# Last unit's stores moved into the else branch of the flag test, and its first copy from ScalarE to VectorE

## The chip, the cores and the metric

The kernel runs on 1 core of one Trainium2 chip. The metric is device time in microseconds (us) of one launch. The kernel before was run four times: 572.84, 571.76, 571.29 and 570.13 us, median 571.53 us.

## The reference

A gated linear recurrence over 768 tokens (4 batches, 8 heads, 48 values a head) feeds a two-layer network with an ELU between the layers. Cut to what is computed:

```python
f = 1.0 / (1.0 + np.exp(-f_logit))
state = np.zeros((B, H, D, D))
for t in range(S):
    state = f[:, :, t, :, None] * state + einsum('bhd,bhe->bhde', k[:, :, t], v[:, :, t])
    y[:, :, t] = einsum('bhd,bhde->bhe', q[:, :, t], state)
x = y.transpose(0, 2, 1, 3).reshape(B * S, H * D)     # 3072 x 384
h = x @ w_in                                          # 384 x 2048
g = np.where(h > 0, h, np.exp(np.minimum(h, 0)) - 1)
out = g @ w_out                                       # 2048 x 384
```

## The kernel before

The 3072 rows of the output are cut into 12 units of 256 tokens (`NU` = 12). `fast` does the whole computation: for each unit the recurrence as chunked matrix products, and then the network in 8 pairs of column blocks (`NP` = 8): `up` makes a pair's hidden values, `elu` the activation, `down` adds the pair's part of the second product into PSUM. The loop at L1134 runs over the steps of all units in an order written out by hand; `down` trails `up` by two pairs (`LAG`). This order stands in a manual schedule that ends with `start.close()` at L1153, behind the last `down`.

From the third unit on both products are done with seven half-size products in the place of eight. For the second product this leaves four PSUM banks (`pm[0]` to `pm[3]`, each 128 x 384, used as two halves of 192), and at a unit's last pair (`j == NP - 1`, L979 to L998) they are put together: ScalarE copies a half of bank 0 into SBUF tile `u2` (L986), and five VectorE additions (the helper at L985, called at L987 to L991) make from it, from the tile `u43` and from the banks the 256 x 384 result `o`. Each addition but the last two uses what the one before wrote. The result goes to DRAM in four stores of 96 KB (L992 to L997), one for each half of the columns of each 128 rows. SyncE's queue issues them; for the last unit the two stores of the second 128 rows go through ScalarE's queue. `o` is a tile of pool `sb` with two buffers, used by the units in turn.

`fast` also checks that its inputs allow its shortcuts. Late in the last unit the check ends in one number, `flag` (L1017 and L1018), 128 when all is well. At L1162 each engine loads it from SBUF into a register, and at L1163 each engine tests it on its own: below 128 the slower kernel `general` runs and writes everything once more; otherwise every engine jumps over `general`'s instructions. L1163 is also the line of the semaphore instructions that follow the jump and bring the engine's semaphores to the values that `general` would have left. L1193 is the end of the program: SyncE waits for every semaphore, all engines meet, and the semaphores are cleared.

What sets the order around the change is each engine's own program order: on an engine, the load of `flag` and the jump stand behind all that `fast` issues on it. For SyncE and ScalarE that includes the last unit's stores.

Of the kernel before, what the change touches and what calls it, by code (L numbers as in the profile page):

```python
# [8 lines left out]
FP32 = mybir.dt.float32  # L9
# [344 lines left out]


@with_exitstack
def fast(ctx: ExitStack, tc: tile.TileContext, q, k, v, f_logit, w_in, w_out, out, flag):

# [15 lines left out]
    nc = tc.nc  # L376
    B, H, D, S = q.shape
    DM = H * D
# [3 lines left out]
    U = 256  # L382
# [3 lines left out]
    NU = B * UPB  # L386
# [5 lines left out]
    DH = DM // 2  # L392
# [22 lines left out]
    sb = ctx.enter_context(tc.tile_pool(name="sb", bufs=2))  # L415
# [54 lines left out]
    for y in first_y:  # L470
# [7 lines left out]
        out=causal[:], in_=causal[:], compare_op=ALU.is_ge, fill=0.0, base=0,  # L478
# [450 lines left out]
    def elu(P):  # L929
# [5 lines left out]
        if m >= DIRECT:  # L935
            s = ss[P] = sb.tile([128, 4, 128], FP32, tag="sums", name=f"sums{m}_{j}", bufs=3)
            a = [[g[:, i, t * 128 : (t + 1) * 128] for i in range(2)] for t in range(2)]
            for i, x, y, op in (
# [2 lines left out]
            ):  # L941
                nc.gpsimd.tensor_tensor(out=s[:, i], in0=x, in1=y, op=op)  # L942

    def down(P):
        m, j = order[P]
        if j == 0:
            pms[m] = [ps.tile([128, DM], FP32, tag=f"m{i + 2 * (m == 1)}", name=f"psM{m}_{i}") for i in range(NW if m < DIRECT else 4)]
        pm, g = pms[m], gs.pop(P)
        ends = dict(start=(j == 0), stop=(j == NP - 1))
        if m < DIRECT:  # L950
            for i in range(2):
                for t in range(NW):
                    nc.tensor.matmul(  # L953
                        pm[t][:], lhsT=g[:, i, t * 128 : (t + 1) * 128], rhs=wo[:, 2 * j + i, :],
                        start=(j == 0 and i == 0), stop=(j == NP - 1 and i == 1),
                    )
            if j == NP - 1:
                o = sb.tile([128, 2, DM], FP32, tag="o", name=f"o{m}")
                for t in range(NW):
                    nc.scalar.copy(o[:, t], pm[t][:])  # L960
                    t0 = m * U + t * 128
                    nc.sync.dma_start(out=out[t0 : t0 + 128, :], in_=o[:, t])
                del pms[m]
            return
        s = ss.pop(P)
        a = [[g[:, i, t * 128 : (t + 1) * 128] for i in range(2)] for t in range(2)]
        b = [[wo[:, 2 * j + i, h * DH : (h + 1) * DH] for h in range(2)] for i in range(2)]
        c = [combos[:, i, j] for i in range(4)]

        for bank, half, x, y in (  # L970
            (0, 0, a[0][0], b[0][0]), (3, 0, a[0][1], b[1][0]), (0, 1, s[:, 1], c[1]),
            (1, 0, s[:, 0], c[0]), (1, 1, s[:, 2], c[2]), (2, 1, a[1][1], c[3]), (2, 0, s[:, 3], b[1][1]),
        ):
            first = j == 0 and (bank, half) in ((0, 0), (3, 0), (1, 0), (2, 1))
            nc.tensor.matmul(  # L975
                pm[bank][:, half * DH : (half + 1) * DH], lhsT=x, rhs=y,
                start=first, stop=(j == NP - 1), skip_group_check=True,
            )
        if j == NP - 1:  # L979
            p = [[pm[i][:, h * DH : (h + 1) * DH] for h in range(2)] for i in range(4)]  # L980
            o = sb.tile([128, 2, DM], FP32, tag="o", name=f"o{m}")
            u2 = sb.tile([128, DH], FP32, tag="u2", name=f"u2_{m}", bufs=1)
            u43 = sb.tile([128, 2, DH], FP32, tag="u43", name=f"u43_{m}", bufs=1)
            flat = o[:].rearrange("p t f -> p (t f)")
            add = lambda to, x, y: nc.vector.tensor_tensor(out=to, in0=x, in1=y, op=ALU.add)  # L985
            nc.scalar.copy(u2[:], p[0][0])  # L986
            add(flat[:, 0:DH], p[3][0], u2[:])  # L987
            add(u2[:], p[0][1], u2[:])
            add(u43[:], pm[1][:].rearrange("p (h f) -> p h f", h=2), u2[:].unsqueeze(1).broadcast_to([128, 2, DH]))
            add(flat[:, 3 * DH :], p[1][0], u43[:, 1])  # L990
            add(flat[:, DH : 3 * DH], pm[2][:], u43[:].rearrange("p h f -> p (h f)"))  # L991
            for t in range(2):  # L992
                for h in ((1, 0) if t else (0, 1)):
                    (nc.scalar if t and m == NU - 1 else nc.sync).dma_start(
                        out=out[m * U + t * 128 : m * U + (t + 1) * 128, h * DH : (h + 1) * DH],
                        in_=o[:, t, h * DH : (h + 1) * DH],
                    )  # L997
            del pms[m]  # L998

    low = cst.tile([128, 1], FP32, name="low")  # L1000
# [107 lines left out]
    for n in range(1, NFT):  # L1108
        t = max(needs[n][0] - 2, 0)
# [12 lines left out]
    for u in range(3, NU):  # L1122
        t = (u - 1) * NFT
# [4 lines left out]
    for n in range(NR):  # L1128
        t = 3 * NFT + (NU - 4) * NFT * n // NR + RR
# [4 lines left out]
    for T in range(NU * NFT):  # L1134
        P = T // 2
        sevens = order[P][0] >= DIRECT
        if T % 2 and sevens:
            joined(P)
        if T % 2 == 0 and P and order[P - 1][0] < DIRECT:
            elu(P - 1)  # L1140
        for f in plan.pop(T, ()):
            f()
        if T % 2 == 0:
            up(P)
        elif P >= LAG:
            down(P - LAG)
        for n in later.pop(T, ()):
            split(n)
            lower(n)
    elu(NU * NP - 1)  # L1150
    for P in range(NU * NP - LAG, NU * NP):
        down(P)
    start.close()  # L1153


def kernel(tc, q, k, v, f_logit, w_in, w_out, out):

    nc = tc.nc
    with tc.tile_pool(name="flags", bufs=1) as pool:
        flag = pool.tile([1, 1], I32, name="flag")  # L1160
        fast(tc, q, k, v, f_logit, w_in, w_out, out, flag)
        seen = nc.values_load(flag[0:1, 0:1])  # L1162
        with tc.If(seen < 128):  # L1163
            general(tc, q, k, v, f_logit, w_in, w_out, out)


# [30 lines left out]
```

## Time and profile before

| what | value |
|---|---|
| median of four runs | 571.53 us (570.13 to 572.84) |
| the profiled execution's own time | 571.99 us |
| its span, first to last instruction | 570.2 us |
| outside the span | 1.8 us |
| granted TensorE clock, mean | 0.979 |
| TensorE busy | 547.7 us (96%) |
| VectorE / ScalarE / GpSimd busy | 394.6 / 229.6 / 265.6 us |
| last matmul ends | about 563.25 us |
| last VectorE addition ends | 564.68 us |
| from there to the end of the span | 5.5 us |

Busy times are sums over the instructions of an engine; the span runs from the first to the last instruction of any engine, and the time of a run is some 1.8 us more. TensorE is busy nearly throughout. Behind its last matmul stand 6.9 us in which it does nothing, and that is where this change is made. The profile does not count branches, semaphore instructions or DMA issues as busy, so these 6.9 us look nearly empty in the busy figures; they are read from the rows of the lines L1162, L1163 and L1193.

### The profile page before, as it was taken

What the parts mean: (1) busy time and instruction counts of PE and PEld (TensorE: products, weight loads), DVE (VectorE), ACT (ScalarE), POOL (GpSimd) and SP (SyncE); (2) the same over time, 40 slices, a digit from 0 to 9 for tenths busy, and PEclk for the clock granted to TensorE, in tenths of its full rate; (3) what the DMA queues carried; (4) which work ended last, traced back from release to release, by engine and by line L of the source; (5) the groups of instructions that cost most, each with busy time, mean ns of one, the idle gap of its engine ahead of it and who ended that gap; (6) DMA issues with size and microseconds to landing.
All of it is one profiled execution on the core that took longest, in us unless ns stands there. A gap on an engine that the chain in (4) does not pass through costs nothing.

```text
span 570.2 us, 15171 instructions
## 1 busy us (share of the span) xinstructions
PE 547.7 (96%) x6210; PEld 503.6 (88%) x6210; DVE 394.6 (69%) x764; ACT 229.6 (40%) x418; POOL 265.6 (47%) x530
## 2 busy tenths in 40 slices
PE   5688999999999999999999999999999999999995
PEld 2566777778999999999999999999999999999994
DVE  8689476745885785885785885885786786745542
ACT  3287736333443443434333343343333433333331
POOL 6510027642374465465366357257257347325332
PEclk9598999999999999999999999999999999999998
DMA  8989770060025224215216216216216202201001
GB/s 204 250 216 307 183 209 14 2 160 29 2 45 137 65 55 142 78 43 152 79 36 155 85 37 152 85 37 153 84 37 154 84 15 65 86 7 30 29 1 35
DMA packets 37902, 53.27 MB, mean 93 GB/s; under 512 B 3680, under 2 KB 27648, under 8 KB 37824
## 3 DMA queue, kind: packets, MB, share of 16 engines
q1 hardware_dynamic: 37024, 51.62, 34.4%
q8 instruction: 51, 0.84, 0.6%
q10 hardware_dynamic: 800, 0.59, 0.4%
q14 instruction: 27, 0.22, 0.1%
HBM read 44.04 MB, written 4.72 MB: 86 GB/s over the span
## 4 chain that ended last, share of the span: by engine, by line
PE 91%; DMA 4%; DVE 2%; POOL 1%; ACT 1%; issue 1%; ACTq 0%; SPq 0%; DVEq 0%; POOLq 0%
PE psH L878 35%; PE psM L975 33%; PE psM L953 8%; PE psH L923 6%; PE psS L701 2%; PE psY L739 2%; PE psY L759 2%; PE psU_a L724 2%; PE psT L665 2%; DMA area<-in_moe_w_in_dram 1%; DMA f<-f 1%; DMA area<-in_moe_w_out_dram 1%; DMA k<-in_k_dram 1%; ACT area L569 1%; DVE bits L559 0%
## 5 line engine op out<-in xcount | busy, mean ns | idle before, releaser
L878 PE MATMUL psH<-xt,wi 128*128 128x128 f32 (+1 forms) x960 | 177.1, 293 | 0.0
L942 POOL TENSOR_TENSOR sums<-gg 128x128 f32<-128x128 f32 x160 | 69.6, 456 | 210.8 <-DVE gg L932 202.5
L878 PEld LDWEIGHTS psH<-xt,wi 128*128 128x128 f32 x960 | 135.9, 192 | 0.8
L910 ACT ACTIVATE gg<-hh 128x512 f32<-128x512 f32 x80 | 50.4, 631 | 205.9 <-DVE hh L900 138.0
L878 PE MATMUL psH<-xt,area 128*128 128x128 f32 x640 | 110.5, 275 | 0.0
L878 PEld LDWEIGHTS psH<-xt,area 128*128 128x128 f32 x640 | 96.9, 192 | 4.1
L887 DVE TENSOR_TENSOR hh<-psH,u 128x256 f32<-128x256 f32 x80 | 33.8, 423 | 88.6 <-ACT u L885 88.6
L975 PE MATMUL psM<-area,sums 128*128 128x192 f32 x480 | 91.2, 326 | 0.0
L975 PEld LDWEIGHTS psM<-area,sums 128*128 128x128 f32 x480 | 80.1, 190 | 0.2 <-POOL sums L942 0.2
L975 PE MATMUL psM<-wo,gg 128*128 128x192 f32 x320 | 68.1, 335 | 0.0
L617 POOL TENSOR_TENSOR k<-k,f 128x256 f32<-128x256 f32 x48 | 39.1, 817 | 60.0 <-DVE f L622 47.2
L627 DVE RECIPROCAL f<-f 128x256 f32<-128x256 f32 x36 | 62.7, 1747 | 1.3
L911 ACT ACTIVATE gg<-gg 128x512 f32<-128x512 f32 x96 | 60.6, 631 | 3.0
L932 DVE SCALAR_TENSOR_TENSOR gg<-gg,hh 128x512 f32<-128x512 f32 x80 | 55.8, 697 | 1.8 <-ACT gg L911 1.8
L975 PEld LDWEIGHTS psM<-wo,gg 128*128 128x128 f32 x320 | 50.2, 190 | 1.9
L900 DVE TENSOR_TENSOR hh<-psH,u43h 128x256 f32<-128x256 f32 (+1 forms) x160 | 49.8, 352 | 2.7
L923 PE MATMUL psH<-xt,wi 128*128 128x256 f32 x192 | 44.5, 382 | 1.3 <-DVE wi L577 1.1
L942 POOL TENSOR_TENSOR sums<-gg,sums 128x128 f32<-128x128 f32 x80 | 42.7, 534 | 6.3
L953 PE MATMUL psM<-wo,gg 128*128 128x384 f32 x128 | 45.2, 497 | 0.0
L885 ACT COPY u<-psH 128x128 f32<-128x128 f32 x80 | 21.1, 263 | 59.3 <-PE psH L878 59.3
L923 PEld LDWEIGHTS psH<-xt,wi 128*128 128x128 f32 x192 | 36.0, 190 | 8.5 <-issue 1.5
L900 DVE TENSOR_TENSOR u43h<-psH,hh 128x256 f32<-128x256 f32 x80 | 33.9, 423 | 13.3 <-PE psH L878 13.0
(96 smaller groups left out, 721.7 us busy)
## 6 DMA issues: line engine op xcount, KB each, us to landing
area<-in_moe_w_out_dram SPq DMA_DIRECT2D x8, 768.0 KB, 8.4
again<-in_moe_w_in_dram SPq DMA_DIRECT2D x16, 384.0 KB, 4.0
again<-in_moe_w_out_dram SPq DMA_DIRECT2D x16, 384.0 KB, 3.4
k<-in_k_dram SPq DMA_DIRECT2D x12, 384.0 KB, 5.0
q<-in_q_dram SPq DMA_DIRECT2D x12, 384.0 KB, 5.6
v<-in_v_dram SPq DMA_DIRECT2D x12, 384.0 KB, 6.0
area<-in_moe_w_in_dram SPq DMA_DIRECT2D x8, 576.0 KB, 7.8
out_dram<-o SPq DMA_DIRECT2D x38, 96.0 KB, 1.7
```

What stands on the lines that cost most here:

```text
L617: e.tensor_tensor(out=t[n][:, p], in0=t[n][:, p], in1=t["f"][:, p, "kq".index(n)], op=ALU.mult)
L627: nc.vector.reciprocal(f[:, p, 1], f[:, p, 0])
L878: nc.tensor.matmul(to, lhsT=lhs, rhs=rhs, start=(n == 0), stop=True, skip_group_check=True)
L887: add = lambda to, x, y: nc.vector.tensor_tensor(out=to, in0=x, in1=y, op=ALU.add)
L900: add = lambda to, x, y: nc.vector.tensor_tensor(out=to, in0=x, in1=y, op=ALU.add)
L910: nc.scalar.activation(g[:], h, AF.Relu, scale=-1.0)
L911: nc.scalar.activation(g[:], g[:], AF.Exp, scale=-1.0)
L923: nc.tensor.matmul(ph[:, i], lhsT=wi[j][:, kt, i * 128 : (i + 1) * 128], rhs=xts[m][:, kt, :], start=(kt == 0), stop=(kt == NKT - 1),)
L932: nc.vector.scalar_tensor_tensor(out=g[:], in0=g[:], scalar=-1.0, in1=phs.pop(P), op0=ALU.add, op1=ALU.max)
L942: nc.gpsimd.tensor_tensor(out=s[:, i], in0=x, in1=y, op=op)
L953: nc.tensor.matmul(pm[t][:], lhsT=g[:, i, t * 128 : (t + 1) * 128], rhs=wo[:, 2 * j + i, :], start=(j == 0 and i == 0), stop=(j == NP - 1 ...
L975: nc.tensor.matmul(pm[bank][:, half * DH : (half + 1) * DH], lhsT=x, rhs=y, start=first, stop=(j == NP - 1), skip_group_check=True,)
```

## The change

Three things are changed.

The four stores of the last unit are no longer issued in `fast`. `down` puts the function that issues them into the list `left`, `fast` returns it, and the program calls it in an else branch of the flag test. The queues are the same: SyncE for the first 128 rows, ScalarE for the second.

The tile `o` comes from two pools of one buffer each, in turn: from `sb` for units with an even number and from the pool that also holds `flag` for odd ones. That pool lives beyond `fast`, and the last unit, number 11, takes its tile from it.

The copy into `u2` goes to VectorE in the last unit; in the others it stays on ScalarE.

```diff
-def fast(ctx: ExitStack, tc: tile.TileContext, q, k, v, f_logit, w_in, w_out, out, flag):
+def fast(ctx: ExitStack, tc: tile.TileContext, q, k, v, f_logit, w_in, w_out, out, flag, outer):
...
+    left = []
...
-            o = sb.tile([128, 2, DM], FP32, tag="o", name=f"o{m}")
+            o = (outer if (NU - m) % 2 else sb).tile([128, 2, DM], FP32, tag="o", name=f"o{m}", bufs=1)
...
-            nc.scalar.copy(u2[:], p[0][0])
+            (nc.vector.tensor_copy if m == NU - 1 else nc.scalar.copy)(u2[:], p[0][0])
...
-            for t in range(2):
-                for h in ((1, 0) if t else (0, 1)):
-                    (nc.scalar if t and m == NU - 1 else nc.sync).dma_start(
-                        out=out[m * U + t * 128 : m * U + (t + 1) * 128, h * DH : (h + 1) * DH],
-                        in_=o[:, t, h * DH : (h + 1) * DH],
-                    )
+            def store(*queues):
+                for t in range(2):
+                    for h in ((1, 0) if t else (0, 1)):
+                        queues[t].dma_start(
+                            out=out[m * U + t * 128 : m * U + (t + 1) * 128, h * DH : (h + 1) * DH],
+                            in_=o[:, t, h * DH : (h + 1) * DH],
+                        )
+
+            if m == NU - 1:
+                left.append(store)
+            else:
+                store(nc.sync, nc.sync)
...
     start.close()
+    return left[0]
...
-        fast(tc, q, k, v, f_logit, w_in, w_out, out, flag)
+        store = fast(tc, q, k, v, f_logit, w_in, w_out, out, flag, pool)
         seen = nc.values_load(flag[0:1, 0:1])
-        with tc.If(seen < 128):
+        with tc.If(seen < 128) as branch:
             general(tc, q, k, v, f_logit, w_in, w_out, out)
+        with branch.Else():
+            store(nc.sync, nc.scalar)
```

More of the change, by code (lines that the diff above doesn't have):

```diff
@@ L980, in down @@
             p = [[pm[i][:, h * DH : (h + 1) * DH] for h in range(2)] for i in range(4)]
-            o = sb.tile([128, 2, DM], FP32, tag="o", name=f"o{m}")
+            o = (outer if (NU - m) % 2 else sb).tile([128, 2, DM], FP32, tag="o", name=f"o{m}", bufs=1)
             u2 = sb.tile([128, DH], FP32, tag="u2", name=f"u2_{m}", bufs=1)
```

## The prediction

> **What bounds the kernel now.** I read the page first, for what fills the span, then the chain of waits of the last 15 us, then single lines and queues there.
>
> ```profile
> span 570.2 us, 15171 instructions
> PE 547.7 (96%) x6210; PEld 503.6 (88%) x6210; DVE 394.6 (69%) x764; ACT 229.6 (40%) x418; POOL 265.6 (47%) x530
> ```
>
> PE is the bound of the kernel up to its last matmul, and nothing in the change touches a matmul. The chain of waits shows where PE's part ends:
>
> ```profile
> 556.22 7.04 PE psM L975 x42
> 563.26 0.57 DVE u L985
> 563.83 0.02 issue
> 563.86 0.37 DVE o L985
> 564.22 0.19 DVEq L1162
> 564.42 0.26 DVE o L985
> ```
>
> Columns are start, length and what ran. The last matmul ends at 563.26 and the last addition at 564.68; the span ends at 570.2. The chain stops 5.5 us early because what follows is not counted as busy. It is the rows of L1162 (load of the flag), L1163 (jump and semaphores behind it) and L1193 (end of the program) that fill this gap:
>
> ```profile
> L1162 SPq TENSOR_LOAD <-flag x1: 491/491/491, 565.1 to 565.1; - x1
> L1162 ACTq TENSOR_LOAD <-flag x1: 577/577/577, 565.3 to 565.3; - x1
> ...
> L1163 SPq EVENT_SEMAPHORE  x8: 17/17/17, 568.2 to 568.8; - x8
> L1163 POOLq COMPARE_BRANCH  x1: 45/45/45, 561.9 to 561.9; - x1
> L1163 PEldq COMPARE_BRANCH  x1: 3962/3962/3962, 562.5 to 562.5; - x1
> L1163 DVEq COMPARE_BRANCH  x1: 72/72/72, 564.5 to 564.5; - x1
> L1163 POOLq EVENT_SEMAPHORE  x1: 17/17/17, 564.5 to 564.5; - x1
> L1163 SPq COMPARE_BRANCH  x1: 50/50/50, 565.7 to 565.7; - x1
> L1163 ACTq COMPARE_BRANCH  x1: 58/58/58, 565.9 to 565.9; - x1
> L1163 PEldq EVENT_SEMAPHORE  x1: 51/51/51, 566.6 to 566.6; - x1
> L1163 DVEq EVENT_SEMAPHORE  x1: 21/21/21, 567.4 to 567.4; - x1
> L1163 ACTq EVENT_SEMAPHORE  x1: 17/17/17, 568.8 to 568.8; - x1
> ...
> L1193 SPq EVENT_SEMAPHORE  x10: 17/28/28, 568.9 to 570.1; - x10
> ```
>
> The figures are durations in ns (lowest, median, highest) and the first and last start. On every engine 2.6 to 4.1 us lie between the start of the jump and the instruction behind it: POOL 561.9 to 564.5, PE 562.5 to 566.6, DVE 564.5 to 567.4, SP 565.7 to 568.2, ACT 565.9 to 568.8. SP is last where it matters: its jump stands behind its last store (issued at 564.71, 0.33 long) and the flag's load (565.09 to 565.58). Behind the gap SP runs 8 semaphore instructions in 0.60, then 8 more (L1193) in 0.57 to 569.42; from there the meeting of the engines and the clearing take 0.75 to 570.17. ACT is through at 568.85, before SP needs it.
>
> What the stores themselves need is in the DMA view of 561 to 571:
>
> ```profile
> out_dram<-o SPq DMA_DIRECT2D x2, 96.0 KB, 2.8
> out_dram<-o ACTq DMA_DIRECT2D x2, 96.0 KB, 2.5
> ```
>
> The last number is us from issue to landing. By their semaphores the two stores of SP are complete at 566.10 and 567.01, those of ACT at 566.62 and 567.27. All have landed 1 us before SP is back from its jump at 568.25: now **the jump hides the landing**, not the reverse.
>
> **The change, part by part.**
>
> *Stores into the else branch.* The issues are the same four, on the same queues, so no instruction is added for them; they move behind the flag's load and the jump. On SP nothing else is queued between the last store of unit 10 (issued at 533.59) and those of unit 11, and the flag is written at 552.2 (its cast is a 136 ns DVE instruction there). So SP loads the flag at about 552.4, jumps at 553.0 and is in the else branch at 553.0 + 2.6 = 555.6, while the first store is due at 562.7. SP's jump (0.55 from the end of its issue to the jump's start, plus 2.6) leaves the end, covered by 7 us of PE work. If that cover were gone it would cost 3.1 us again. Nothing is queued behind the waiting stores on SP but the end of the program.
>
> On ACT the last activation of the last unit starts at 558.10; the load of the flag (0.58) and the jump can follow, and ACT would be back at about 558.1 + 0.6 + 2.8 = 561.5 to 562.1, whether the load goes beside the activation or behind it. Its first store is due at 564.24. This works only because of the copy's move: with the copy still on ACT (561.99 to 562.31) ACT would be back at 562.0 + 0.6 + 2.8 = 565.4 or later, 1.2 us too late.
>
> PE, POOL and DVE issue no stores; their jumps stay where they are. DVE's is now next in line: it starts at 564.49, DVE is back at 567.40 and ready for the meeting at 567.51.
>
> *The tile in an outer pool.* Two pools of one buffer, used in turn, are the same rotation as one pool of two. No instruction, no wait: 0.
>
> *The copy on VectorE.* Before, ACT's copy starts at 561.99 and the addition waiting for it at 562.34: 0.35. The trace has no DVE copy of 128x192 from PSUM. From below, DVE's cast of one element took 0.136; from above, its addition of 128x192 took 0.358. Between dependent DVE instructions there are 0.105 (562.695 to 562.800). So 0.24 to 0.46 in the place of 0.35. A copy moves as many elements as the addition, so I take 0.45, near the upper row: the whole chain of additions shifts by **+0.10** (bounds -0.11 and +0.11), and the last addition ends at 564.78. DVE was idle for 2.46 us before, so the copy delays no other work.
>
> The row for ACT's copy is 0.300 (median of ten). [...]
>
> *The end.* The last stores are issued at 564.81 (SP) and about 564.84 (ACT). From issue to landing: the last two took 2.30 and 2.53 in this trace; over all 38 stores of SP the median is 1.7. In the before the landing shares the DMA engines with instruction transfers around 565.1 to 567.1, of which SP's and ACT's are gone now, so I take 2.1, between the ends: landed at 566.9 (566.5 to 567.4). SP has done the semaphores that do not depend on the stores; behind the last landing come some 0.3 of the first eight (0.1 to 0.6), 0.57 for the second eight, and 0.75: 566.9 + 0.3 + 0.57 + 0.75 = **568.5**. From below, DVE's late jump sets 567.51 + 0.10 + 0.75 = 568.35, whatever the stores do. From above, 567.4 + 0.6 + 0.57 + 0.75 = 569.3. I take 568.6, since both ends of the sum meet DVE's bound from above.
>
> [...]
>
> The sum: span 570.2 - 1.6 + 0 = 568.6, bounds 568.35 (-1.8) and 569.3 (-0.9). I use -1.5, a little to the side of the upper bound, because a late landing costs in full and an early one nothing. The profiled execution would take 571.99 - 1.5 = 570.5. It lies 0.46 above the median of its runs, so against the median 571.53 - 1.5 = **570.0 us**.
>
> About 0.3% (1.7 us) is what a measurement of this kernel can tell from no change: its four runs are spread over 2.7 us.
>
> **The rivals.**
>
> *Two jumps in series.* If the end of the else branch does not run on into the end of the program but needs code that is fetched only then, every engine stands still twice. For: each engine shows a gap of 2.6 to 4.1 us at a jump. Against: behind the one jump L1163 and L1193 follow each other within 0.1 us on all engines. Price: DVE 567.51 + 0.10 + 2.9 = 570.5, PE 566.73 + 4.1 = 570.8; plus 0.75 is 571.3 to 571.6, +1.1 to +1.4: **572.8 us**. It decides from the point where the second gap exceeds about 1.7 us on DVE.
>
> *A wait ahead of the jump (slower).* If the branches are treated as a unit, SP waits for the last addition before it tests the flag. Then load, jump and landing stand in series: 564.80 + 0.55 + 2.6 = 567.95, the second store 0.4 later at 568.35, landing 1.7 to 2.5 later at 570.1 to 570.9, then 0.3 + 0.57 + 0.75: 571.7 to 572.5, +1.5 to +2.3, so **573.4 us**. It decides as soon as SP's load of the flag starts after about 562.5. Against it: POOL jumps at 561.9 and PE at 562.5, while DVE and PE still use the memory that `general` would write; waits of the branch's content stand inside, not ahead.
>
> *Little is left.* The gain is taken back by something late: ACT's return after 564.3, or a gap at the end of SP's else branch. For: ACT's gap of 2.8 has a margin of only 2.1 to 2.7 us. Price: between -0.5 and +0.5, **571.5 us**.
>
> **How the numbers follow.** The forecast (-0.9 to -1.8) has a chance of 0.72, little is left 0.08, two jumps 0.10, a wait ahead 0.10. Its 1.5 us is just under the 1.7 us that count as a difference, and a median of a few runs moves by some 0.5 us, so half of the 0.72 falls on faster: 0.36. Same: 0.36 + 0.08 + half of the two jumps = 0.49. Slower: 0.05 + 0.10 = 0.15. The forecast's own range, with 0.5 for the runs, is 569.2 to 571.1. The whole range reaches over little is left and the start of two jumps, 569.0 to 572.5, and leaves out the wait ahead and most of the two jumps.
>
> **What would show it.** Right: L1162 and L1163 on SP at 552 to 553 and on ACT near 559; the four stores on the else branch's line, issued at 562.8 to 564.9; SP's semaphores of L1163 and L1193 in one run behind a landing near 567; the span's end 0.75 behind the later of SP and DVE. Wrong: the flag's load on SP at 564 or later (a wait ahead), a second gap on DVE or PE behind the first (two jumps), ACT's stores after 564.4 (little is left), or a changed time at a place before 560.

## The result and the profile after

The changed kernel takes 569.85 us (median of 52 runs, 567.85 to 571.98), the kernel before 571.54 us in the same comparison (78 runs). The ratio is 0.9971, with a 95% interval of 0.9964 to 0.9978: 1.7 us less, between 1.3 and 2.1. Over this many runs that is clear of the scatter; by the bound of 0.3% (1.7 us) that the prediction set it is just inside no change.

The profiled execution has a span of 567.3 us, 2.8 less than the 570.2 before. Not all of that belongs to the change: the last unit's first copy starts at 560.67 in the place of 561.99, 1.3 us earlier, with a granted clock of 0.986 in the place of 0.979. Ahead of that copy the change moves nothing but SyncE's and ScalarE's loads of the flag and jumps; in e9 below they are moved in the same way, and there the copy starts at 562.10. Over the other profiles below, which have the same work up to that copy apart from loads of the flag and jumps, it starts between 559.93 and 563.43. So the two kernels are compared **from the start of that copy to the end of the span**: 8.18 us before, 6.67 after, 1.51 less. All times below that say "after the copy" are measured from there.

The chain of waits of the changed kernel shows the same end of TensorE and a chain of VectorE work of the same length. Columns are start, length and what ran:

```profile
554.91 5.74 PE psM L977 x34
...
560.67 0.37 DVE u L988
561.04 0.02 issue
561.07 0.37 DVE o L987
561.43 0.02 issue
561.46 0.37 DVE u L987
...
561.92 0.57 DVE u L987
...
562.51 0.37 DVE o L987
562.88 0.19 DVEq L1174
563.07 0.26 DVE o L987
```

From the copy's start to the end of the last addition it is 2.66 us (2.69 before). The gain of 1.5 us therefore lies behind the last addition: 5.49 us before, 4.01 after. The rows of the flag's load (now L1174) and of the test (now L1175) say why, with durations in ns and the first and last start in us:

```profile
L1174 SPq TENSOR_LOAD <-flag x1: 473/473/473, 551.1 to 551.1; - x1
L1174 ACTq TENSOR_LOAD <-flag x1: 475/475/475, 556.8 to 556.8; - x1
...
L1175 SPq EVENT_SEMAPHORE  x4: 17/17/17, 563.7 to 564.0; - x4
L1175 SPq COMPARE_BRANCH  x1: 45/45/45, 551.6 to 551.6; - x1
L1175 ACTq COMPARE_BRANCH  x1: 54/54/54, 557.3 to 557.3; - x1
...
L1175 DVEq COMPARE_BRANCH  x1: 72/72/72, 563.1 to 563.1; - x1
...
L1175 DVEq EVENT_SEMAPHORE  x1: 21/21/21, 566.3 to 566.3; - x1
```

SyncE (SP) loads the flag at 551.1 and jumps at 551.6; before, both stood behind its last store, 14 us later. It is in the else branch at 554.34, ScalarE (ACT) at 559.85, and both then wait for VectorE's result. The gap of SP's jump, 2.7 us, is still there; it lies beside TensorE's work. What SP waits for at the end is in its own waits, of the changed kernel from 550 on (total, times, longest):

```profile
SPq L997 <- DVE o L987: 8.4, 2, 7.0
...
SPq L1207 <- DMA out_dram<-o: 1.9, 2, 1.2
...
SPq L1207 <- DVEq L1175: 0.2, 1, 0.2
```

The landing of the stores (1.9) and then VectorE's return from its jump (0.2) have taken the place of SP's own jump as what ends last. The two lie close together: the last store lands 5.44 us after the copy, VectorE is back at 5.65.

### The profile page after: what moved, and what is told of

Its sections match the earlier page's. It is cut to its first block, busy times and chain, and to the rows that moved or that the text cites. A ratio compares the mean times of both kernels' runs of the same rounds, so it can differ in the third digit from the quotient of the medians.

```text
span 567.3 us, 15170 instructions
## 1 busy us (share of the span) xinstructions
PE 546.1 (96%) x6210; PEld 501.7 (88%) x6210; DVE 395.1 (70%) x765; ACT 229.2 (40%) x417; POOL 265.4 (47%) x530
## 4 chain that ended last, share of the span: by engine, by line
PE 91%; DMA 4%; DVE 2%; issue 1%; ACT 1%; SPq 0%; POOL 0%; DVEq 0%; ACTq 0%; POOLq 0%
PE psH L878 35%; PE psM L977 33%; PE psM L955 8%; PE psH L923 6%; PE psS L701 2%; PE psY L739 2%; PE psY L759 2%; PE psU_a L724 2%; PE psT L665 2%; DMA area<-in_moe_w_out_dram 1%; DMA area<-in_moe_w_in_dram 1%; DMA f<-f 1%; DVE f L627 1%; DMA f<-in_f_logit_dram 0%; ACT area L569 0%
```

## The experiments

The theory: the whole gain is that SP and ACT jump while they have nothing else to do. The rivals: that the copy, the tile's other pool, or the stores' new place in the order make it. Behind that the question is what binds the end now. The table gives the profiled execution of each kernel, in us after the copy, and the ratio to the kernel before with its 95% interval. "Back" is the first instruction behind the jump.

| kernel | SP back | VectorE back | last landing | end | ratio |
|---|---|---|---|---|---|
| before | 6.26 | 5.41 | 5.29 | 8.18 | 1 |
| changed | -6.33 | 5.65 | 5.44 | 6.67 | 0.9971 (0.9964 to 0.9978) |
| e1 copy alone | 6.57 | 5.65 | 5.48 | 8.49 | 1.0000 (0.9986 to 1.0014) |
| e2 copy back on ScalarE | -6.55 | 5.41 | 7.99 | 9.06 | 1.0005 (0.9990 to 1.0019) |
| e3 stores ahead of the test | 6.17 | 5.43 | 5.31 | 8.09 | 0.9996 (0.9983 to 1.0008) |
| e4 load ahead of the stores | 6.55 | 5.35 | 5.18 | 8.47 | 1.0000 (0.9989 to 1.0011) |
| e5 no test | none | none | 4.63 | 5.88 | 0.9955 (0.9940 to 0.9971) |
| e6 all stores on SyncE | -6.55 | 5.62 | 5.92 | 6.96 | 0.9976 (0.9959 to 0.9993) |
| e7 flag loaded early | -6.19 | 4.96 | 6.25 | 7.32 | 0.9959 (0.9944 to 0.9974) |
| e9 VectorE's jump late | -6.55 | 6.80 | 5.17 | 7.82 | 0.9989 (0.9977 to 1.0001) |
| e10 changed, again | -6.55 | 5.40 | 5.19 | 6.42 | 0.9979 (0.9966 to 0.9992) |
| e11 as e7, again | -6.13 | 4.96 | 5.19 | 6.26 | 0.9966 (0.9948 to 0.9984) |

**e1, the copy alone.** The kernel before with one line changed:

```diff
-            nc.scalar.copy(u2[:], p[0][0])
+            (nc.vector.tensor_copy if m == NU - 1 else nc.scalar.copy)(u2[:], p[0][0])
```

> The kernel before with the last unit's copy on VectorE and nothing else. Theory (the end is set by SyncE's jump behind its stores): from the copy's start to the end of the span 8.1 to 8.2 us, as in the kernel before (8.18), and a ratio of 1.000 within 0.001. Rival (the copy's move or a shorter chain of additions is the gain): about 6.7 us, as in the changed kernel, and a ratio near 0.997.

No gain. The end is 0.3 us later than in the kernel before because SP's gap was 2.94 us in this execution in the place of 2.60; over all the profiles here SP's gap lies between 2.50 and 2.94.

**e3, the stores ahead of the test.** Tile, copy and function `store` of the changed kernel, in another order:

```diff
+        store(nc.sync, nc.scalar)
         seen = nc.values_load(flag[0:1, 0:1])
-        with tc.If(seen < 128) as branch:
+        with tc.If(seen < 128):
             general(tc, q, k, v, f_logit, w_in, w_out, out)
-        with branch.Else():
-            store(nc.sync, nc.scalar)
```

> The changed kernel with the same stores, tile and copy, but the stores issued ahead of the flag's load and test. Theory (the place behind the jump is the whole gain): 8.1 to 8.2 us from the copy's start to the end, ratio 1.000 within 0.001. Rival (the tile's other pool and place, or the stores' place behind the hand-made order): 6.7 us, ratio near 0.997.

8.09 us and 0.9996: the gain is gone, with everything of the change there but the order. The rows of the test, now L1176, are those of the kernel before:

```profile
L1176 SPq EVENT_SEMAPHORE  x8: 17/17/17, 567.7 to 568.2; - x8
L1176 SPq COMPARE_BRANCH  x1: 50/50/50, 565.1 to 565.1; - x1
L1176 ACTq COMPARE_BRANCH  x1: 58/58/58, 565.4 to 565.4; - x1
```

SP jumps 3.63 us after the copy and is back at 6.17. With e1 this settles the rivals: neither the copy, nor the other pool, nor the new place of the stores behind `fast` is worth anything that the runs can show; the stores must stand behind the jump.

**e4, the load ahead of the stores.** Meant to part the load's 0.5 us from the jump's 2.6:

```diff
         seen = nc.values_load(flag[0:1, 0:1])
-        with tc.If(seen < 128) as branch:
+        store(nc.sync, nc.scalar)
+        with tc.If(seen < 128):
             general(tc, q, k, v, f_logit, w_in, w_out, out)
-        with branch.Else():
-            store(nc.sync, nc.scalar)
```

> The changed kernel with the flag's load first, then the stores, then the test. Theory: SyncE jumps right behind its last store, so the load's 0.55 us are saved and the gap of the jump of 2.6 us remains: 7.5 to 7.7 us from the copy's start to the end, ratio 0.999. Rival (the load's wait is the larger part): under 7.2 us.

Missed, because the edit didn't do what it says. In the built program the load stands behind the stores on both engines, as its rows show, 3.07 us after the copy on SP:

```profile
L1174 SPq TENSOR_LOAD <-flag x1: 487/487/487, 563.3 to 563.3; - x1
L1174 ACTq TENSOR_LOAD <-flag x1: 614/614/614, 563.5 to 563.5; - x1
```

So e4 is e3 once more, with the same result. What the load alone costs there stays open; no kernel that parts the two was run.

**e2, the copy back on ScalarE.** The changed kernel with the copy's line as it was before.

> The changed kernel with the last copy back on ScalarE. Theory: ScalarE loads the flag only behind the copy, is back from its jump about 3.5 us after the copy's start, 1.2 us late for its first store; its second store starts about 4.0 us after the copy's start in the place of 2.8, lands 2.6 later, and the end comes 7.7 to 7.9 us after the copy's start (before 8.18, changed 6.67): a gain of 0.3 to 0.5 us, ratio 0.999. Rival (only SyncE's jump counts): 6.7 us, ratio 0.997.

ScalarE is back 3.51 us after the copy, as expected, and its first store begins at 3.64, 1.4 us later than in the changed kernel. But the loss is larger than expected: 9.06 us from copy to end, and a ratio of 1.0005, all of the gain. The rows of the stores in e2 show where the rest is:

```profile
L997 ACTq DMA_DIRECT2D out_dram<-o x2: 688/1439/2190, 565.6 to 568.0; - x2
```

and in the changed kernel:

```profile
L997 ACTq DMA_DIRECT2D out_dram<-o x2: 401/421/441, 562.9 to 563.5; - x2
```

The first store takes 2.19 us to issue in the place of 0.40, the second 0.69 in the place of 0.44, so the second lands at 7.99. What may be behind this is taken up in the last section. The move of the copy is worth nothing by itself (e1) and is needed for the gain as soon as ScalarE has stores to issue.

**e6, all four stores on SyncE,** with the copy on ScalarE:

```diff
-            (nc.vector.tensor_copy if m == NU - 1 else nc.scalar.copy)(u2[:], p[0][0])
+            nc.scalar.copy(u2[:], p[0][0])
...
-            store(nc.sync, nc.scalar)
+            store(nc.sync, nc.sync)
```

> The changed kernel with all four stores on SyncE and the copy back on ScalarE. Theory (ScalarE's late jump costs only through its stores): SyncE issues the last store about 3.7 us after the copy's start in the place of 2.8 on ScalarE, lands 2.5 later, end 7.2 to 7.5 us after the copy (before 8.18, changed 6.67, copy back alone 9.06), ratio 0.9985. Rival (ScalarE must be through its jump early by itself, as every engine meets at the end): 8 us or more.

6.96 us, somewhat better than expected, and a ratio of 0.9976, whose interval overlaps that of the changed kernel. ScalarE is back just as late as in e2 (3.56), and nothing waits for it: the end is 1.04 us behind the last landing. It is through its stores that ScalarE's jump counts. SyncE issues the last two stores at 3.17 and 3.82, and the last landing is at 5.92.

**e9, VectorE's jump late.** Two more additions behind the last one of the changed kernel, into `u43`, which nothing reads any more:

```diff
             add(flat[:, DH : 3 * DH], pm[2][:], u43[:].rearrange("p h f -> p (h f)"))
+            if m == NU - 1:
+                for _ in range(2):
+                    add(u43[:], pm[1][:].rearrange("p (h f) -> p h f", h=2), u2[:].unsqueeze(1).broadcast_to([128, 2, DH]))
```

> The changed kernel with two more VectorE additions (128x384, 0.55 us each, into a tile that nothing reads) behind the last one, so that VectorE's jump starts 1.1 us later and no store does. Theory (VectorE's jump binds the end): VectorE is back about 6.7 us after the copy and the end comes at 7.7 to 7.8, ratio 0.999. Rival (the landing binds, VectorE has room): 6.7 to 6.9.

VectorE comes back 1.15 us later than in the changed kernel (6.80 against 5.65), and the end comes 1.15 us later (7.82 against 6.67). In both, and in e10, the end is 1.02 us behind VectorE's return. The last landing is even earlier here (5.17). The rows of VectorE's jump and SP's wait for its return in e9:

```profile
L1178 DVEq COMPARE_BRANCH  x1: 72/72/72, 566.0 to 566.0; - x1
L1178 DVEq EVENT_SEMAPHORE  x1: 21/21/21, 568.9 to 568.9; - x1
...
SPq L1210 <- DVEq L1178: 1.6, 1, 1.6
```

So in these executions VectorE's jump binds the end, in the changed kernel by no more than the 0.2 us that SP waits for it behind the last landing. The ratio, 0.9989, says the same: most of the gain is given back.

**e5, no test.** The flag's load, its test and `general` are left out; the stores stand behind `fast`.

```diff
-        seen = nc.values_load(flag[0:1, 0:1])
-        with tc.If(seen < 128) as branch:
-            general(tc, q, k, v, f_logit, w_in, w_out, out)
-        with branch.Else():
-            store(nc.sync, nc.scalar)
+        store(nc.sync, nc.scalar)
```

> The changed kernel with the flag's load, its test and general left out, the stores issued behind fast. It leaves the check of the inputs out of account. Theory (what is left of the test in the changed kernel is VectorE's jump, level with the landing): the end is set by the last landing alone, 4.9 to 5.4 us after the copy's start, plus 0.45 and 0.75: 6.1 to 6.6 us from copy to end (changed 6.67, before 8.18), ratio 0.996 to 0.997. Rival (the jump still costs over 1 us in the changed kernel): under 5.6 us.

5.88 us, below what the theory expected and above the rival. It gives the price of the whole test: 8.18 - 5.88 = 2.3 us before, 6.67 - 5.88 = 0.8 in the changed kernel (0.5 in its second profile, e10). The 0.2 that the theory missed is in the landing. The DMA view of e5, from 560 to 570, issue to landing in us last:

```profile
out_dram<-o SPq DMA_DIRECT2D x2, 96.0 KB, 1.6
out_dram<-o ACTq DMA_DIRECT2D x2, 96.0 KB, 1.8
```

and of the changed kernel in the same stretch:

```profile
out_dram<-o SPq DMA_DIRECT2D x2, 96.0 KB, 2.9
out_dram<-o ACTq DMA_DIRECT2D x2, 96.0 KB, 2.5
```

Store by store it is 1.62 to 1.91 us in e5 and 2.44 to 3.31 in the changed kernel: the same four stores land 0.7 to 1.7 us sooner where no engine jumps. Each of the four completes in 16 parts, by the updates of its semaphore. In e5 the 14th part of the last store comes at 4.60 after the copy and the last at 4.63; in the changed kernel at 4.92 and 5.44. Beside the late parts stand transfers that bring instructions: between 561 and 566 the changed kernel has five of them, 8 or 16 KB each, and e5 none. That these transfers are what makes the parts late is inferred; e5 shows that the delay goes with the test.

**e7 and e11, the flag loaded early; e10, the changed kernel beside it.** The load follows the flag's making by two steps; the test stays where it is.

```diff
     at_step((NU - 1) * NFT + 13, lambda: finish_flag(1))
+    at_step((NU - 1) * NFT + 15, lambda: left.append(nc.values_load(flag[0:1, 0:1])))
...
-    return left[0]
+    return left
...
-        store = fast(tc, q, k, v, f_logit, w_in, w_out, out, flag, pool)
-        seen = nc.values_load(flag[0:1, 0:1])
+        seen, store = fast(tc, q, k, v, f_logit, w_in, w_out, out, flag, pool)
```

> The changed kernel with the flag's load on each engine right behind the flag's making, two steps later, instead of directly ahead of the test. Theory (VectorE's jump is the next bound, level with the landing): VectorE's jump starts some 0.5 us earlier, it is back about 5.1 us after the copy in the place of 5.65, and the landing at 5.4 sets the end: 6.4 to 6.6 us, ratio 0.997. Rival (the landing alone binds): 6.67 unchanged; a rise over 6.8 would say that the load stops an engine earlier.

VectorE is back at 4.96 in the place of 5.65, as expected. But in this execution one part of ScalarE's second store lands at 6.25 (its 14th at 4.75), and the end is 7.32. The times speak the other way: 0.9959. So it was run again, with the changed kernel beside it:

> The changed kernel once more, beside the next run on the same chip. Ratio to the kernel before 0.996 to 0.998; 6.6 to 7.0 us from the copy's start to the end of the span.

> The early load of the flag once more, beside the changed kernel on the same chip. If VectorE's and TensorE's jumps, 0.6 and 0.8 us earlier, are worth something: 0.1 to 0.5 us under the changed kernel, and a single late landing of the one profile before (6.25 us after the copy) does not recur. If the landing alone binds: the same time within 0.2 us, and 6.5 to 7.3 us from copy to end again.

The late part does not recur (5.19), and from copy to end it is 6.26 us, against 6.42 for the changed kernel and 5.88 without any test. The medians are 569.54 and 570.30 us, but the intervals of their ratios overlap widely. That the early load beats the kernel before is shown twice; that it beats the changed kernel is likely and not shown.

## Why the prediction was right

The time, 570.0 us, was 0.15 too high, and the gain of 1.5 us is the 1.51 of the profile and close to the 1.7 of the medians. The mechanism was right: SP's and ACT's jumps leave the end, and VectorE's becomes the next bound. That the size agrees so closely is partly luck. Counted from the copy, the last landing was forecast at 4.91 us and came at 5.44, what follows it was 0.4 shorter than forecast, and VectorE's return, which the sum took as a bound from below, came later than forecast and ended last.

- *SP's jump leaves the end.* Right in kind and size: loading the flag, jumping and being in the else branch were forecast for 552.4, 553.0 and 555.6 and found at 551.1, 551.6 and 554.3, earlier by the 1.3 us by which everything was earlier. e3 shows that this order is what counts. One reading was off: from the end of the last store's issue to the jump's start it was 0.61 us before, not 0.55; only the price without the cover rests on it.
- *ACT in time only with the copy moved.* Right for stores on ACT's queue: back 3.0 us ahead of its first store (forecast 2.1 to 2.7). It loads the flag beside its last activation (both start at 556.79), not behind it. e6, with all stores on SP, keeps most of the gain without the move. The price without this cover was put at 1.2 us; e2 lost 2.4 from copy to end, since the late store also took 1.8 us longer to issue.
- *The tile at nothing.* Not told apart alone; with the copy and the stores' new place it is nothing within 0.2% (e3: 0.9983 to 1.0008).
- *The copy, +0.10.* Off in size and sign, within its bounds: the chain came out 0.03 shorter. The copy itself took 0.357 us, close to the upper row, as was taken. But no separate semaphore instruction stands between the first and the second addition any more, and the gap there shrank from 0.105 to 0.035: from the copy's start to the end of the last addition it is 2.66 in all the kernels with this copy, in the place of 2.69. In the rows of the changed kernel VectorE's copy is 0.057 longer than ScalarE's median:

```profile
L988 ACT COPY u<-psM x9: 299/300/301, 179.5 to 528.7; 128x192 f32<-128x192 f32 x9
L988 DVE COPY u<-psM x1: 357/357/357, 560.7 to 560.7; 128x192 f32<-128x192 f32 x1
```

- *The landing, 2.1 us.* Mis-sized: 2.52 and 2.63 for the last two stores, at and above the upper bound. The reason given was that with SP's and ACT's transfers gone the DMA engines would be freer. Two transfers are indeed gone, which in the kernel before began 0.9 us behind the jumps of SP and ACT, and five are left while GpSimd, TensorE and VectorE jump. The last two stores gained nothing by it: 2.30 and 2.53 before, 2.52 and 2.63 here, 2.27 and 2.38 in e10. Without any jump (e5) they take 1.65 and 1.91.
- *Behind the landing, 0.3 + 0.57 + 0.75.* Mis-sized the other way: 1.23 in the place of 1.62. The first eight semaphores had all been dealt with before the landing (two by ACT and two by SP ahead of their stores, four by SP at 563.7 to 564.0), and of the second eight only the last four were left, 0.47 with what follows. In these 0.47 SP stands 0.2 for VectorE; where the landing alone ends last, the end is 1.04 to 1.07 behind it (e6, e7, e11).
- *VectorE as the next bound.* Right, and a little worse than forecast: SP waits for VectorE's semaphore ahead of its own last steps, so the end is 1.02 us behind VectorE's return and not 0.86; its gap was 3.18 us in the place of 2.90.

Of the rivals, no second gap showed behind the first on any engine, and no engine waited for the else branch's needs ahead of its jump: SP and ACT jumped 9.05 and 3.34 us before the copy.

## What to carry to other kernels

In these kernels the test of a value on the chip cost each engine its own gap at the jump, 2.5 to 4.2 us, and what counted was where in each engine's program order it fell: SyncE and ScalarE, which could test early and do their last work inside the branch, hid gaps of 2.7 and 2.5 us beside the others' work. Look for what else stands ahead of the test on such an engine, as the small copy did on ScalarE (e2: 1.4 us late), and for the engine that has to work to the end and can't test early, as VectorE here: its gap, 3.18 us, became the new end. To compare such tails, measure from the same event in both profiles, since the spans differed by almost twice the effect.

## What the runs showed of the hardware

In three profiles the long DMA issues are nearly all beside transfers that bring instructions. In the kernel before, 8 DMA issues took over 1 us, and 7 of these overlap a 16 KB instruction transfer; of the 219 that took under 0.7 us, 15 do. In the changed kernel it is 6 of 6 against 18 of 219, in e3 6 of 6 against 15 of 222. The 2.19 us issue of a store in e2, at 565.64 to 567.83, overlaps one that begins at 567.15, with four smaller ones around it. By then 1.51 us of the issue had passed, so this transfer can't be the whole reason there; that store is also issued 0.13 us behind ScalarE's return from its jump, against 3.05 in the changed kernel. That the transfers make the issues long is an inference; it was not tried by moving one of them, and for e2 the cause stays open.

The gap at the jump differs between the profiles: SP 2.50 to 2.94, VectorE 2.86 to 3.18, TensorE 3.45 to 4.16 us. Two executions of the changed kernel already differ: 2.72 and 2.50 (e10) on SP, 3.18 and 2.93 on VectorE.
